# Gated linear attention and a SiLU block on one core: y of the first chunks by halves of the heads, the turnings of k behind the next chunk's, and a Silu and a sum one place later

## The chip, the cores and the metric

The kernel runs on one core of one Trainium2 chip. The time is that of one execution on the device in microseconds, taken as the median of the runs shown. Profiles show one execution each: TensorE (PE, and PEld for its weight loads), VectorE (DVE), ScalarE (ACT), GpSimd (POOL), and the DMA queues that SyncE (SP) and POOL issue.

## The reference

Two blocks follow each other. The first is a linear attention with a decaying state, for 4 batches, 8 heads, 768 steps and a head width of 48:

```python
for t in range(S):
    state = alpha[:, :, t, :, None] * state + np.einsum('bhd,bhe->bhde', k[:, :, t], v[:, :, t])
    y[:, :, t] = np.einsum('bhd,bhde->bhe', q[:, :, t], state)
```

Its y, laid out as 3072 tokens by 384, is x of the second block, with w_in of 384 x 2048 and w_out of 2048 x 384:

```python
h = x @ w_in
g = h * (1.0 / (1.0 + np.exp(-h)))
return (g @ w_out).astype(np.float32)
```

alpha and the weights arrive as 64-bit floats; everything is computed in fp32.

## The kernel before, in words

**Work and its tiles.** The sequence is cut into chunks of 128 steps, so there are 24 chunks n: 6 pieces of time (ci) by 4 batches (b). Chunks 0 to 3 are the first time piece (ci == 0): they have no earlier state to read. Four chunks make a group of 512 tokens for the second block; there are six groups.

**Attention of a chunk.** `bring` turns alpha, k and q with TensorE (`pe.transpose` against the identity, four per operand) into PSUM; the alpha part is copied by ACT (`al`, L759), the other two stay in PSUM. `products` and `quotient` (DVE) scan alpha in both directions and scale k and q by the running products, which gives `kp` and `qp`. `scores` multiplies them into two PSUM banks, one for the even and one for the odd head of each pair (u = 0, 1); ACT copies each bank to `g` (L854), and POOL zeroes what lies in the future with a select (L855), u = 0 first, then u = 1. `back` turns `kp` back (four transposes into a PSUM bank, an ACT copy to `kn`, L891). `values` computes y from `g` and v in 16 products with 32 columns of weights each, into one PSUM bank, and, where ci > 0, adds 12 products of the state with `qp`; ACT copies the bank to `xt` (L913), which is x of the second block. `states` multiplies `kn` with v into the new state; ACT copies it (L932) for ci == 0, DVE adds it otherwise (L930), and `scores` of the next time piece scales the old state on ACT (L874, four instructions).

**PSUM.** `ps_attn` hands out three banks in turn. `scores` takes two of them, `back`, `bring` (alpha), `values` and `states` one each; a bank is free again when its reader is done.

**Weights.** The 64-bit weights come in pieces (12 of w_in, then 16 of w_out), fetched by SP into four buffers `bits`. Converting a piece takes one ACT instruction (`up`, L654) and three of DVE (L670, L672, L673), after which the next piece is fetched. `convert(0, upto)`, in `start` shortened to `w(upto)`, converts pieces of w_in up to that count. The `up` of a piece is made with the piece before it, except that of the twelfth.

**Second block.** `enter_plain` computes four blocks of tokens of h directly, for the first two groups. From group 2 on, `enter(grp, pair)` computes a pair with a scheme of 20 block products (SUMS_X, SUMS_W, PRODUCTS) that are combined by DVE with additions and subtractions (L1008), over three PSUM banks a, b, c and a single SBUF buffer `part`, and ACT applies Silu in four instructions (L1005), each to two parts of a `g` tile. `leave` multiplies by w_out in seven products per half group (L1137 to L1163), with sums on DVE and stores L1115 and L1117.

**What sets the order.** The attention stages of step n and pieces of the second block are interleaved by hand: `start` writes out chunks 0 to 3, a loop with `fill` does the rest, calling `go_on` for one piece of second-block work at a time. Within that, TensorE's instructions keep the order of the program from the start to the end. DVE, ACT and POOL have theirs set by the framework's scheduler, except where `settled` or `tc.keep_in_program_order` pins an instruction. In `audit`, reductions over alpha and the weights (L723) are spread over the whole run on DVE; each waits for its own DMA.

**Lines that the texts below use.** `scores` calls `back(n)` at its end for n != 1 (L869); for chunk 1 `start` calls it after `values(0)`. The part of `start` for chunks 2 and 3 reads, shortened:

```python
scores(2); w(8); bring(3); w(9); values(2); states(2)
...
scores(3); bring(4); load(NIN + 4); w(12); values(3); states(3)
```

In `enter`, pair 0 of group 4 already has two orders of its own: `late_2` puts the subtraction from `s[2]` (L1050), which reads `part`, behind the addition to `s[6]`, and `late_3` one further subtraction behind its successor.

Of the kernel before, what the change touches and what calls it, by code (L numbers as in the profile page):

```python
# [355 lines left out]
def quotients(  # L356
# [237 lines left out]
    def combine(to, sa, a, sb, b):  # L594
        if sa == sb == 1:
            return dve.tensor_tensor(to, a, b, ALU.add)
        if sa == 1:
            return dve.tensor_tensor(to, a, b, ALU.subtract)
        if sb == 1:
            return dve.tensor_tensor(to, b, a, ALU.subtract)  # L600
        return dve.scalar_tensor_tensor(to, a, -1.0, b, ALU.mult, ALU.subtract)
# [227 lines left out]
    def scores(n):  # L829
        c = ctxs[n]  # L830
        ci, b = c["ci"], c["b"]
        ps = [ps_attn() for _ in range(2)]

        for j in (0, 2, 1, 3):
            for e in range(2 if n >= NA else 1):
                for u in range(2):
                    r = slice(64 * u, 64 * u + D)
                    at = slice(CH * e, CH * e + CH) if n >= NA else slice(0, C)  # L840
                    t = slice(CH * (e ^ j // 2) if n >= NA else 0, C)
                    pe.matmul(ps[u][at, j, t], lhsT=c["kp"][r, j, at], rhs=c["qp"][r, j, t],
                              start=True, stop=True)
        if n == 1:

            room = gpool.tile([128, 4, 2, TB], F32, name="g").rearrange("p a b n -> p (a b n)")
            c["room"] = room[:, 2 * NP * C :]
        g = (room[:, 0 : 2 * NP * C] if n == 1 else decayed).rearrange(
            "p (u j c) -> p u j c", u=2, j=NP)
        swapped = decayed.rearrange("p (o u j c) -> p o u j c", o=2, u=2, j=NP // 2)  # L850
        c["g"] = (lambda u, j: g[:, u, j, :]) if n < NA else (
            lambda u, j: swapped[:, j // 2, u, j % 2, :])
        for u in range(2 if n < NA else 0):
            settled(act.copy(g[:, u], ps[u]))  # L854
            gps.affine_select(g[:, u], g[:, u], pattern=[[0, NP], [1, C]], compare_op=ALU.is_ge,  # L855
                              fill=0.0, base=0, channel_multiplier=-1)
        if n >= NA:
            ps = [x.rearrange("p (o j) c -> p o j c", o=2) for x in ps]
            for u in range(2):
                act.copy(swapped[:, :, u, :, CH:], ps[u][:, :, :, CH:])  # L860
            for r, o in earlier:
                for u in range(2):
                    act.copy(swapped[r, o, u, :, 0:CH], ps[u][r, o, :, 0:CH])
            for at, half in ((CH, later), (0, earlier)):
                for r, o in half:
                    x = swapped[r, o].rearrange("p u j c -> p (u j) c")[:, :, at : at + CH]
                    gps.affine_select(x, x, pattern=[[0, NP], [1, CH]],  # L867
                                      compare_op=ALU.is_ge, fill=0.0, base=0, channel_multiplier=-1)
        if n != 1:  # L869
            back(n)  # L870
        if ci > 0:
            s = st[b].rearrange("p j u e -> p j (u e)")
            for j in range(NP):
                mul = act.mul(s[:, j], s[:, j], least[:, n, j : j + 1])  # L874
                if late or n == 6:
                    tc.keep_in_program_order(mul)
# [4 lines left out]
    def back(n):  # L881

        c = ctxs[n]
        if n >= NA or c["ci"] == NCH - 1:
            return
        ps_k = ps_attn()
        for j in range(NP):
            pe.transpose(ps_k[:, j, :], c["kp"][:, j, :], ident)
        c["kn"] = c.pop("room")[:, 0 : NP * C].rearrange("p (j c) -> p j c", j=NP) if (
            "room" in c) else work.tile([128, NP, C], F32, name="kn")  # L890
        settled(act.copy(c["kn"], ps_k))  # L891

    def values(n):

        c = ctxs[n]
        ci, b, g, qp = c["ci"], c["b"], c.pop("g"), c["qp"]
        vn = c["v"].rearrange("p (j u) d -> p j (u d)", u=2)
        s = st[b].rearrange("p j u e -> p j (u e)")
        py = ps_attn()
        todo = [(3 * j + i, vn[:, j, at : at + 32], g(u, j))  # L900
                for j in range(NP) for i, at, u in ((0, 0, 0), (1, 32, 0), (2, 80, 1))]
        todo += [(3 * j + 1, vn[:, j, 48:80], g(1, j)) for j in range(NP)]
        if ci > 0:
            todo += [(3 * j + i, s[:, j, 32 * i : 32 * i + 32], qp[:, j, :])
                     for j in range(NP) for i in range(3)]
        for i, (at, w, x) in enumerate(todo):
            t, at = divmod(at, 4)
            pe.matmul(py[32 * at : 32 * at + 32, t, :], lhsT=w, rhs=x, start=(i < 4),
                      stop=(i >= len(todo) - 4), skip_group_check=True)
        half, e = divmod(n, 2)  # L910
        if e == 0:
            xts[half] = xtp.tile([128, NKT, TB], F32, name="xt")
        settled(act.copy(xts[half][:, :, e * C : (e + 1) * C], py[:, 0:NKT]))  # L913
# [67 lines left out]
    def enter(grp, pair):  # L981
        g_tiles(grp, pair)
        halves = [gts[grp, h, pair] for h in range(2)]

        s = [halves[o % 2][:, o // 2] for o in range(8)]
        todo = iter(PRODUCTS)

        def new(i):
            return bank(i).rearrange("p (e n) -> p e n", e=2)

        def add(ps, first=False):
            w, x = next(todo)
            for e in range(2):
                pe.matmul(ps[:, e], lhsT=block_w(w)[:, 2 * pair + e], rhs=block_x(grp, x),
                          start=(first and e == 0), stop=(e == 1), skip_group_check=True)

        def copy(ps, to=None):
            if to is None:
                to = late["part"].tile([128, 2, TB], F32, name="part")
            act.copy(to, ps)  # L1000
            return to

        def silu(h, i):
            x = halves[h][:, i : i + 2]
            act.activation(x, x, AF.Silu)  # L1005

        def tt(to, a, b, op=ALU.add):
            dve.tensor_tensor(to, a, b, op)  # L1008

        a, b, c = [new(i) for i in range(3)]  # L1010
        add(a, True)
        copy(a, s[6])
        add(b, True)
        copy(b, s[2])
        add(c, True)
        tt(s[6], s[6], copy(c), ALU.subtract)
        yield
        add(c)
        copy(c, s[7])
        add(b)  # L1020
        copy(b, s[4])
        add(a)
        tt(s[7], s[7], copy(a), ALU.subtract)
        yield
        add(a)
        copy(a, s[5])
        add(b)
        copy(b, s[3])
        tt(s[5], s[5], s[3])
        add(c)  # L1030
        copy(c, s[0])
        yield
        add(a)
        tt(s[4], a, s[4])
        b = new(1)
        add(b, True)
        add(b)
        copy(b, s[1])
        yield
        c = new(2)  # L1040
        add(c, True)
        t = copy(c)
        late_2 = (grp, pair) == (4, 0)
        if not late_2:
            tt(s[2], s[2], t, ALU.subtract)
        a = new(0)
        add(a, True)
        tt(s[6], a, s[6])
        if late_2:
            tc.keep_in_program_order(dve.tensor_tensor(s[2], s[2], t, ALU.subtract))  # L1050
        silu(0, 2)
        add(b)
        tt(s[5], copy(b), s[5], ALU.subtract)
        yield
        add(c)
        tt(s[1], c, s[1])
        late_3 = (grp, pair) in ((2, 0), (4, 0))
        if not late_3:
            tt(s[3], s[1], s[3], ALU.subtract)
        a = new(0)  # L1060
        add(a, True)
        tt(s[2], a, s[2])
        if late_3:
            tt(s[3], s[1], s[3], ALU.subtract)
        add(b)
        tt(s[7], b, s[7])
        silu(1, 2)
        yield
        add(c)
        combine(s[1], -1, s[1], -1, s[0])  # L1070
        tt(s[0], c, s[0])
        silu(0, 0)
        a = new(0)
        add(a, True)
        tt(s[3], a, s[3])
        silu(1, 0)
        turn.append(turn.pop(0))
        for h in range(2):
            side_by_side(grp, h, pair)
        yield  # L1080
# [180 lines left out]
    def start():  # L1261
# [34 lines left out]
        scores(2)  # L1296
        w(8)
        bring(3)
        w(9)
        values(2)  # L1300
        states(2)
# [5 lines left out]
        w(11)  # L1307
        go_on()
        scores(3)
        bring(4)  # L1310
        load(NIN + 4)
        w(12)
        values(3)
        bridged = 4
        states(3)
# [120 lines left out]
```

## Time and profile before

| | us |
|---|---|
| median of three runs | 551.8 (551.37 to 552.56) |
| the profiled execution | 552.26 |
| its span, first to last instruction | 550.5 |
| PE busy | 539.8 |
| PEld busy | 493.0 |
| DVE busy | 446.3 |
| ACT busy | 209.1 |
| POOL busy | 79.7 |

By stretch, the busy time of PE is 46.0 of the first 50 us, 74.5 of the next 75, all of the 259 from 125 to 384, 14.8 of the 16 from 384 to 400, and 145.5 of the last 150.5. The granted TensorE clock is full throughout (0.999 in the mean).

How to read the lines: a row of the timeline has the start in us from the span's first instruction, the length, the engine, the line of the kernel, the operation, output <- inputs, the shapes and how many instructions are merged (x4). In square brackets stands the time for which the engine was idle before it, with what ended that wait; "issue" means that nothing in the profile ended it. A line of the view of waits has the waiting engine and line, what it waited for, and then the total in us, the number of waits and the longest. One fp32 product of TensorE appears as two records, each a weight load (LDWEIGHTS, on PEld) and a MATMUL (on PE). The operation of the helper that records all products has one line, L394, and that of the transposes L398; they are told apart by their tiles.

### The profile page before, as it was taken

What the parts mean: (1) busy time and instruction counts of PE and PEld (TensorE: products, weight loads), DVE (VectorE), ACT (ScalarE), POOL (GpSimd) and SP (SyncE); (2) the same over time, 40 slices, a digit from 0 to 9 for tenths busy, and PEclk for the clock granted to TensorE, in tenths of its full rate; (3) what the DMA queues carried; (4) which work ended last, traced back from release to release, by engine and by line L of the source; (5) the groups of instructions that cost most, each with busy time, mean ns of one, the idle gap of its engine ahead of it and who ended that gap; (6) DMA issues with size and microseconds to landing.
All of it is one profiled execution on the core that took longest, in us unless ns stands there. A gap on an engine that the chain in (4) does not pass through costs nothing. (4 is left out here: it accounts for less than half of the span.)

```text
span 550.5 us, 12714 instructions
## 1 busy us (share of the span) xinstructions
PE 539.8 (98%) x5068; PEld 493.0 (90%) x5068; DVE 446.3 (81%) x801; ACT 209.1 (38%) x466; POOL 79.7 (14%) x146
## 2 busy tenths in 40 slices
PE   8899999999999999999999999999999999999996
PEld 7788888998999899899999999998798999999996
DVE  5998789986989899997998986998884796945531
ACT  3655654213333433444444344353263341332100
POOL 4111001221222102201111111021121000001000
PEclk9999999999999999999999999999999999999999
DMA  9999761355445434545445653816732135500000
GB/s 214 301 238 221 205 187 43 87 147 138 109 119 138 116 96 107 131 127 157 123 133 157 166 147 90 219 33 152 192 126 85 54 100 166 172 11 19 13 29 26
DMA packets 99218, 70.11 MB, mean 127 GB/s; under 512 B 56272, under 2 KB 88656, under 8 KB 99152
## 3 DMA queue, kind: packets, MB, share of 16 engines
q1 hardware_dynamic: 97232, 65.30, 45.7%
q0 software_dynamic: 1920, 3.93, 2.0%
q8 instruction: 41, 0.67, 0.5%
q14 instruction: 25, 0.20, 0.1%
HBM read 61.34 MB, written 7.86 MB: 126 GB/s over the span
## 5 line engine op out<-in xcount | busy, mean ns | idle before, releaser
L394 PE MATMUL ps_o<-w_out,g 128*128 128x192 f32 x768 | 133.7, 328 | 0.6 <-DVE o L1117 0.6
L394 PEld LDWEIGHTS ps_o<-w_out,g 128*128 128x128 f32 x768 | 125.8, 190 | 3.1 <-DVE o L1117 0.8
L394 PE MATMUL ps_m<-xt,w_in 128*128 128x256 f32 x480 | 111.7, 381 | 0.9 <-ACT xt L913 0.5
L394 PEld LDWEIGHTS ps_m<-xt,w_in 128*128 128x128 f32 x480 | 89.7, 190 | 13.6 <-ACT part L1000 0.8
L394 PE MATMUL ps_o<-wt,g 128*128 128x192 f32 x576 | 99.7, 326 | 0.0
L394 PEld LDWEIGHTS ps_o<-wt,g 128*128 128x128 f32 x576 | 95.1, 190 | 1.5
L394 PE MATMUL ps_m<-xc,w_in 128*128 128x256 f32 x288 | 70.7, 382 | 0.0
L394 PEld LDWEIGHTS ps_m<-xc,w_in 128*128 128x128 f32 x288 | 53.7, 190 | 6.9 <-DVE g L1008 0.2
L1005 ACT ACTIVATE g<-g 128x1024 f32<-128x1024 f32 x32 | 33.1, 1056 | 66.1 <-DVE g L1008 66.0
L1108 DVE TENSOR_TENSOR g<-g 128x512 f32<-128x512 f32 x72 | 49.9, 704 | 7.9 <-PE ps_o L394 7.9
L867 POOL TENSOR_SCALAR_AFFINE_SELECT g<-g 64x256 f32<-64x256 f32 x64 | 36.9, 576 | 123.5 <-ACT g L860 104.5
L1120 POOL DMA_DIRECT2D out_dram<-o x40 | 22.0, 551 | 216.2 <-DVE o L1117 111.5
L1000 ACT COPY g<-ps_m 128x512 f32<-128x512 f32 x64 | 36.9, 586 | 41.4 <-PE ps_m L394 41.3
L394 PE MATMUL ps_m<-xc,wx 128*128 128x256 f32 x192 | 50.0, 383 | 0.0
L1008 DVE TENSOR_TENSOR g<-ps_m,g 128x512 f32<-128x512 f32 x56 | 37.3, 683 | 3.2 <-PE ps_m L394 2.7
L394 PEld LDWEIGHTS ps_m<-xc,wx 128*128 128x128 f32 x192 | 35.2, 190 | 4.0 <-issue 0.4
L770 DVE TENSOR_TENSOR_SCAN u<-al,one 128x516 f32<-128x516 f32 x24 | 29.7, 1239 | 7.0 <-ACT al L759 6.7
L973 ACT ACTIVATE g<-ps_m 128x512 f32<-128x512 f32 x32 | 19.0, 595 | 38.0 <-PE ps_m L394 37.7
L800 DVE TENSOR_TENSOR_SCAN p<-al,inv 128x516 f32<-128x516 f32 x24 | 30.2, 1260 | 0.9 <-PE ps_a L394 0.2
L723 DVE TENSOR_REDUCE seen<-bits 128x1 f32<-128x512 int32 (+1 forms) x33 | 26.3, 824 | 5.4 <-DMA bits<-in_moe_w_in_dram 5.4
L1117 DVE TENSOR_TENSOR o<-ps_o,u 128x192 f32<-128x192 f32 x24 | 8.5, 354 | 26.7 <-PE ps_o L394 24.8
L1000 ACT COPY part<-ps_m 128x512 f32<-128x512 f32 x32 | 18.9, 589 | 26.0 <-PE ps_m L394 21.0
(137 smaller groups left out, 655.7 us busy)
## 6 DMA issues: line engine op xcount, KB each, us to landing
bits<-in_moe_w_in_dram SPq DMA_DIRECT2D x24, 512.0 KB, 4.8
bits<-in_moe_w_out_dram SPq DMA_DIRECT2D x16, 384.0 KB, 3.8
at<-in_alpha_dram SPq DMA_DIRECT2D x64, 96.0 KB, 2.7
kt<-in_k_dram SPq DMA_DIRECT2D x64, 96.0 KB, 2.7
qt<-in_q_dram SPq DMA_DIRECT2D x64, 96.0 KB, 2.8
bits<-in_alpha_dram SPq DMA_DIRECT2D x9, 512.0 KB, 4.2
out_dram<-o POOLq DMA_DIRECT2D x40, 96.0 KB, 2.4
flips<-turn SPq DMA_DIRECT2D x12, 256.0 KB, 2.6
```

The source lines that it names most:

```text
L394: in_order(nc.tensor.matmul(*args, **kw))
L723: dve.tensor_reduce(seen[kind][which][:, i : i + 1], x, axis=AX, op=op, apply_absolute_value=True))
L770: settled(dve.tensor_tensor_scan(u[:, end - 1 :: -1], sg[:, end:0:-1], one[:, end:0:-1], 0.0, ALU.mult, ALU.add))
L800: settled(dve.tensor_tensor_scan(p[:, 0:end], sg[:, 0:end], iv[:, 0:end], 0.0, ALU.mult, ALU.add))
L867: gps.affine_select(x, x, pattern=[[0, NP], [1, CH]], compare_op=ALU.is_ge, fill=0.0, base=0, channel_multiplier=-1)
L973: settled(act.activation(gts[grp, h, pair][:, i : i + 2, q % 2, :], ps, AF.Silu))
L1000: act.copy(to, ps)
L1005: act.activation(x, x, AF.Silu)
L1008: dve.tensor_tensor(to, a, b, op)
L1108: dve.tensor_tensor(cells(grp, h, pair, *to), cells(grp, h, pair, *x), cells(grp, h, pair, *y), ALU.subtract)
L1117: dve.tensor_tensor(o, x, y, ALU.add)
L1120: (gps if grp < NG - 1 else nc.sync).dma_start(out[r : r + C, c * HO : (c + 1) * HO], o)
```

## The change

Four edits, in the diff below.

1. `values`, for ci == 0: the 16 products of y are listed anew. The parts are the same (for each of four pairs of heads j: columns 0, 32, 48 and 80 of v, the first two with g of u = 0, the last two with g of u = 1), but the eight of u = 0 come first, then the eight of u = 1. Four products in a row still go to four different quarters of the bank's rows.
2. `scores` no longer calls `back` for chunks 1, 2 and 3. `start` calls `back(2)` behind `bring(3)`, and `back(3)` behind `bring(4)`; chunk 1 is as it was.
3. In `start`, `w(12)` moves from behind `load(NIN + 4)` to ahead of `bring(4)`.
4. In `enter`, for group 4, pair 0 alone: the first Silu (of `s[4]` and `s[6]`) comes behind the copy of bank b and the subtraction from `s[5]` instead of ahead of them, and it and the sum into `s[1]` (`combine`, L601) are pinned to the order of the program.

How the instructions stand on each engine afterwards, from the two built programs:

- PE: in chunks 2 and 3 the four transposes of `kp` come behind the twelve of the next chunk's alpha, k and q. The products of y are in their new order. Nothing else differs.
- ACT: in chunk 2, `up`, `al`, `kn` instead of `kn`, `up`, `al`; in chunk 3, `up`, `al`, `kn` instead of `kn`, `al`, `up`, and of the four scalings of the state (L874) that came behind chunk 3's copies, one now stands ahead of the `xt` copy (L913) and one behind it. In group 4, pair 0, the copy to `part` comes ahead of the first Silu.
- DVE: in group 4, pair 0, L601 comes behind the transpose of alpha (L734) and a store's addition (L1117) instead of ahead of both. Near 55 us, one L1091 and one L672 change places.
- SP: one fetch of w_out comes ahead of the three loads of `load(NIN + 4)` instead of behind them.
- POOL: the same.

```diff
@@ scores
-        if n != 1:
+        if not 1 <= n <= 3:
             back(n)
@@ values
         todo += [(3 * j + 1, vn[:, j, 48:80], g(1, j)) for j in range(NP)]
+        if ci == 0:
+            at = (0, 32, 48, 80)
+            todo = [(3 * j + (i + 1) // 2, vn[:, j, at[i] : at[i] + 32], g(i // 2, j))
+                    for j, i in ((0, 0), (0, 1), (2, 0), (1, 0), (1, 1), (3, 0), (3, 1), (2, 1),
+                                 (0, 3), (0, 2), (1, 2), (3, 3), (1, 3), (2, 3), (2, 2), (3, 2))]
@@ enter
         def silu(h, i):
             x = halves[h][:, i : i + 2]
-            act.activation(x, x, AF.Silu)
+            return act.activation(x, x, AF.Silu)
...
         if late_2:
             tc.keep_in_program_order(dve.tensor_tensor(s[2], s[2], t, ALU.subtract))
-        silu(0, 2)
+        else:
+            silu(0, 2)
         add(b)
         tt(s[5], copy(b), s[5], ALU.subtract)
+        if late_2:
+            tc.keep_in_program_order(silu(0, 2))
         yield
...
         add(c)
-        combine(s[1], -1, s[1], -1, s[0])
+        total = combine(s[1], -1, s[1], -1, s[0])
+        if late_2:
+            tc.keep_in_program_order(total)
         tt(s[0], c, s[0])
@@ start
         bring(3)
+        back(2)
         w(9)
...
         scores(3)
+        w(12)
         bring(4)
+        back(3)
         load(NIN + 4)
-        w(12)
         values(3)
```

## The prediction

> **What bounds the kernel.** The page's first part comes first: TensorE's rows are busy for all but 2% of the span, so only time in which PE issues nothing can be won.
>
> ```profile
> PE 539.8 (98%) x5068; PEld 493.0 (90%) x5068; DVE 446.3 (81%) x801; ACT 209.1 (38%) x466; POOL 79.7 (14%) x146
> ```
>
> The chain that ended last shows one line of DVE and stops, so it does not help. I go to the view of waits (who waited, for whom: total us, times, longest) and look for PEld, the weight loads, with which PE's queue stops.
>
> ```profile
> PEld ps_a L394 <- POOL g L855: 1.3, 3, 0.7
> PEld ps_m L394 <- DVE g L1008: 1.0, 3, 0.6
> PEld ps_o L394 <- DVE o L1117: 0.8, 1, 0.8
> PEld ps_m L394 <- ACT part L1000: 0.8, 1, 0.8
> PEld ps_a L398 <- ACT g L854: 0.7, 2, 0.4
> ```
>
> These five are what the change can touch: 4.6 us, a ceiling. Two places hold nearly all of it: the start (18 to 47 us) and group 4, pair 0 (387 to 396 us). The timeline shows each. Chunk 2, weight loads (start, length, what; in brackets the idle time before and its releaser):
>
> ```profile
> 34.22 0.42 PEld L398 LDWEIGHTS ps_a<-ident,an 128*128 128x128 f32 x4 [0.38 <-ACT g L854]
> ...
> 35.68 0.14 PEld L394 LDWEIGHTS ps_a<-g,vn 128*32 128x32 f32 x4 [0.17 <-issue]
> 36.17 0.69 PEld L394 LDWEIGHTS ps_a<-g,vn 128*32 128x32 f32 x26 [0.35 <-POOL g L855]
> ...
> 36.87 0.58 PEld L394 LDWEIGHTS ps_a<-vn,kn 128*32 128x32 f32 x30
> ```
>
> Each fp32 product shows as two records, so y of a chunk is 32 records. Four are issued (35.68), then PE waits for the second half of the heads (the second select on POOL), and 28 are left behind that wait.
>
> **The change, part by part, against the profiled execution's own 552.26 us (span 550.5).**
>
> *1. Order of y, chunks 0 to 3.* Same 16 products, same columns of PE in turn; the eight of the first half come first, so 16 records instead of 28 stand behind the second select. An undisturbed y (394.00 to 394.90) issues 32 records in 0.90 us: 12 fewer are worth 0.34. Chunk 0 had no wait there: 0. Chunk 1 gains 0.34 at 18.3, but see its next stall:
>
> ```profile
> 20.21 0.23 PEld L394 LDWEIGHTS ps_a<-vn,g 128*32 128x32 f32 x13 [0.81 <-issue]
> ```
>
> That stall lies inside one tile's products, where no data can be late. If PE waits there for something that comes at a fixed time, the 0.34 turns into more waiting. The bounds are 0 and 0.34; I take 0, because the stall (0.81) is longer than the gain.
> The Trainium skill ("Runtime: NRT & Kernel Launch", section "Instruction fetch mechanics") says an engine's instructions are fetched ahead in 16 KiB blocks and that this is hidden by the pace of issue. If it holds here the stall is something else and may move along, making the sum 0.34 better; the 0.81 us of "issue" speaks against it.
>
> *2. Turnings of k (four transposes, one ACT copy) behind those of the next chunk, in chunks 2 and 3.* The 0.30 us that `an` lost waiting for a bank (34.22 against about 33.92) goes. Alone this buys nothing: what is late next is the second select at 36.12. PE now reaches the second half at about 35.8 and waits until 36.17 as before. Chunk 2 gains the 0.34 of part 1 only. ACT now has `up`, `al`, `kn` where it had `kn`, `up`, `al`: kn ends at about 36.2 instead of 35.15, and the states, its readers, start at about 36.6: covered by 0.4.
>
> *3. Chunk 3 arrives 0.34 earlier, and here the select can move.* Timeline, DVE and POOL:
>
> ```profile
> 44.08 0.69 DVE L673 CUSTOM_DVE_ANT_0 w_in<-w_in,up 128x1024 uint16<-128x1024 uint16 x1
> 44.69 0.42 DVE L670 TENSOR_SCALAR w_in<-bits 128x512 int32<-128x512 int32 x1
> 44.78 1.85 POOL L855 TENSOR_SCALAR_AFFINE_SELECT g<-g 128x512 f32<-128x512 f32 x2 [8.67 <-ACT g L854]
> 45.14 1.00 DVE L672 SCALAR_TENSOR_TENSOR w_in<-bits,w_in 128x512 int32<-128x512 int32 x1
> ...
> 45.55 1.08 POOL L855 TENSOR_SCALAR_AFFINE_SELECT g<-g 128x512 f32<-128x512 f32 x1
> ```
>
> L672 takes 1.00 here and 0.69 at 41.36; the selects of chunk 2 take 0.85 and 1.08 (34.23, 35.04) and those of 62.05, where DVE does nothing, 0.61 a piece. So they hold each other off in turn. From these rows: a held-off select ends 0.49 after the DVE instruction (46.63 after 46.14; 36.12 after 35.62), a held-off L672 0.54 after the select (35.62 after 35.08). DVE's own order here comes unbroken from 36.21 and does not move. In the new kernel the first select asks at 44.44, inside L673 and before L670. Whoever asked first goes first (at 94.52 the select waits for L619 and goes ahead of L620), so: select 1 ends 44.77 + 0.49 = 45.26, L670 0.27 later (0.42 less the 0.15 of overlap) at 45.53, select 2 at 46.02 instead of 46.63. PE, without the 0.30 and 0.34 earlier, is at the second half at about 46.0, resumes at 46.08 instead of 46.69 (0.61), with 0.34 less behind it: by the states PE is 0.95 ahead, chunk 2's share included. kn ends at about 46.4, just ahead of the states at 46.5. If DVE goes first instead, select 2 ends at 46.63 again, and 0.34 remains of the 0.95.
> The Trainium skill ("SBUF — State Buffer", section "Who interferes with whom") calls this an exclusive lock between the two engines, held for the whole instruction by whoever issues first. By that rule the select, asking first, gives 0.95; the row at 16.29, where a select and an L670 start together and L670 goes ahead, would leave 0.34.
>
> *4. What else moves there.* Piece 12 of w_in (three DVE instructions, one `up`) is written ahead of chunk 4's turnings; its `up` ends earlier, its last DVE instruction at about 47.4 instead of 47.48; PE's first use of that piece is at about 47.9. A fetch passes load(6) on SP's queue (three DMAs, an at 45.46, up to 1.3 later): chunk 6 is turned only after 77, free. In ACT's order one scaling of the state (L874, waits for DVE L773, 48.66) now stands ahead of the copy of x of chunk 3, which goes from 47.81 to about 49. PE reads that half in the middle of its 10.6 us block from 48.03, near 53: 3 us of cover; past it, each us costs one.
>
> *5. Pair 0 of group 4.* Timelines of PEld, DVE and ACT:
>
> ```profile
> 388.61 0.73 PEld L394 LDWEIGHTS ps_m<-xt,w_in 128*128 128x128 f32 x4 [0.83 <-ACT part L1000]
> ...
> 396.30 2.57 PEld L394 LDWEIGHTS ps_o<-w_out,g 128*128 128x128 f32 x16 [0.84 <-DVE o L1117]
> ```
>
> ```profile
> 386.91 0.68 DVE L1050 TENSOR_TENSOR g<-g,part 128x512 f32<-128x512 f32 x1
> ...
> 394.35 0.68 DVE L601 SCALAR_TENSOR_TENSOR g<-g 128x512 f32<-128x512 f32 x1
> 394.95 1.11 DVE L734 STREAM_TRANSPOSE al<-at 128x512 f32<-128x512 f32 x1
> 395.91 0.34 DVE L1117 TENSOR_TENSOR o<-ps_o,u 128x192 f32<-128x192 f32 x1
> ```
>
> ```profile
> 387.99 0.57 ACT L1000 COPY part<-ps_m 128x512 f32<-128x512 f32 x1
> ...
> 404.06 0.60 ACT L1000 COPY part<-ps_m 128x512 f32<-128x512 f32 x1
> ```
>
> The Silu no longer stands ahead of the copy at 387.99; what is late next is the single `part` buffer, free when L1050 ends (387.59). The copy starts at about 387.65, PE resumes at 388.27: 0.34, which PE carries only to the next wait, L1117. In DVE's new order L601 comes after L734 and L1117. L601 to L734 is a pitch of 0.60, so L1117 ends at 395.65, PE resumes at 395.71: 0.60 in all, the 0.34 inside it. L601's reader (L1008, 397.30) keeps its place, and so does the Silu's (L1091, 399.53). Then ACT: Silu, copies and scalings run without a pause from 398.00 to 404.67, started by DVE and not by PE. The bank that the copy at 404.06 frees is wanted by PE at 405.23; moved up by 0.60 it would be 404.63, but it comes free at 404.72, and the first load is no longer hidden (0.10). Left: 405.23 - 404.72 - 0.10 = 0.41. From 405.43 on ACT waits for PE again.
>
> **Sum:** 0.95 + 0.41 = 1.36: 550.9 for such an execution. The median of the runs shown (551.8) lies 0.46 below the profiled one, so the forecast for the median is **550.4**. From 48 to 384 I assume the shift is kept: PE shows no long wait there, and DVE's idle times end on PE (339.24: 2.24 us).
>
> **Rivals** (as medians). About 0.2%, 1.1 us or 550.7, is what a measurement of this kernel can tell from no change.
> - *DVE goes first in chunk 3.* For it: at 16.29 a select and an L670 start together and L670 wins. Against: here the select asks 0.2 us ahead. 0.34 + 0.41 = 0.75: 551.05.
> - *The stall at 20.2 moves along.* For it: its row names no releaser. Chunk 1's 0.34 then reaches chunk 2, whose select gets ahead of L670 as in part 3 (about 0.15 more): 1.85, 549.95.
> - *The early gain is eaten later* (or part 5 is): DVE, not PE, sets the pace up to 387, so an earlier PE only waits longer at L1008 (387.05). Against: DVE idles for PE at 339 to 341. 0.41 or 0.95 left: 551.4 or 550.85.
> - *Slower.* If the 0.81 at 20.2 is PE running out of instructions after a dense run (83 weight loads from 17.16), then y and states of chunks 2 and 3, now denser, stop likewise: 2 x 0.81 - 1.36 = +0.26, 552.05 (three stops: 552.9). It decides once a run is denser than chunk 1's. Against: 66.76 to 68.77 has 88 loads in 2 us and no stop.
>
> **Chances.** Forecast 0.45, DVE first 0.16, stall moves along 0.17, eaten later 0.13, slower 0.09. The forecast lies only 0.3 below the bound, so a third of it ends within 0.2%: faster 0.30 + 0.17 + 0.04 from the two middling cases = 0.51; slower beyond 0.2% needs the three stops, half of its case, 0.05; same 0.44. The range goes from the second rival less 0.4 (spread of the medians) to the third's upper value plus 0.2: 549.5 to 551.6.
>
> **What would show it.** Right: no PEld wait on ACT L854 at 34 and 44 us; y split 16/16 records around the select; chunk 3's second select ending near 46.0; L1117 ahead of L601 and PE resuming near 395.7 less the early shift; PE 1.3 us earlier from 405 on. Wrong: a select longer than before, PEld waits on kn (L891), new stalls by "issue", or PE's wait at 387.05 grown by the early gain.

## The result, and the profile after

| | before | after |
|---|---|---|
| median of 22 runs each, us | 551.88 (551.18 to 553.04) | 551.15 (550.52 to 553.07) |
| ratio, 95% interval | | 0.9985 (0.9978 to 0.9992) |
| a second time, both on one chip (e5 below): median | 551.12 | 550.11 |
| ratio, 95% interval | | 0.9982 (0.9973 to 0.9991) |
| the profiled execution; its span | 552.26; 550.5 | 551.14; 549.4 |

The change gains 0.7 to 1.0 us, under 0.2%. That is less than the 1.36 of the forecast, and by the bound set there it is "no change", though it stands clear of the noise. The kernel before has medians 0.7 apart on two chips (551.81 and 551.12 below), so below a time is set against those of the same chip alone, and across chips only ratios are compared.

The page's first part of the kernel after, and its view of waits (who waited, for whom: total us, times, longest):

```profile
PE 539.0 (98%) x5068; PEld 491.6 (89%) x5068; DVE 447.4 (81%) x801; ACT 208.7 (38%) x466; POOL 79.1 (14%) x146
```

```profile
PEld ps_a L394 <- issue: 13.0, 44, 1.4
...
PEld ps_a L394 <- POOL g L855: 1.2, 3, 0.6
...
PEld ps_a L398 <- ACT g L854: 0.8, 1, 0.8
...
PEld ps_o L394 <- DVE o L1127: 0.6, 1, 0.6
...
PEld ps_m L394 <- ACT part L1005: 0.5, 2, 0.3
```

(Lines from 903 on have moved by 5 to 10: L1117 is L1127, L1000 is L1005, L1008 is L1013.) In the view of waits before, the first of these rows was:

```profile
PEld ps_a L394 <- issue: 11.9, 43, 0.8
```

The two short waits for L854 have become one long one, L1127 and `part` are shorter, and the longest wait by "issue" has grown from 0.8 to 1.4. Where they lie, in the timeline of weight loads after:

```profile
33.52 0.42 PEld L398 LDWEIGHTS ps_a<-ident,an 128*128 128x128 f32 x4
...
35.42 0.81 PEld L394 LDWEIGHTS ps_a<-g,vn 128*32 128x32 f32 x32 [0.17 <-issue]
...
45.20 0.38 PEld L394 LDWEIGHTS ps_a<-g,vn 128*32 128x32 f32 x16 [0.17 <-POOL g L855]
46.20 0.38 PEld L394 LDWEIGHTS ps_a<-g,vn 128*32 128x32 f32 x16 [0.62 <-POOL g L855]
...
62.43 0.42 PEld L398 LDWEIGHTS ps_a<-ident,an 128*128 128x128 f32 x4 [0.77 <-ACT g L854]
```

`an` of the next chunk no longer waits at 34. Chunk 2's y runs through without any wait for the select (32 records, no cut), chunk 3's is cut 16 and 16, as meant. The long wait for L854 is new: it stands in chunk 4, at 62.43, where the kernel before had none.

To see where PE gains and loses, take the start of the same matmul in two traces; the difference is PE's **lead**. The columns are the places, in us of the trace of before; the values are in us against that trace (minus is earlier, a lead; the runs e1 to e12 come below). "First at 34" says which of two instructions started first in chunk 2, the select on POOL or DVE's L670:

| trace | first at 34 | 16 | 25 | 58 | 70 | 384.5 | 397 | 410 |
|---|---|---|---|---|---|---|---|---|
| after | POOL | -0.16 | +0.09 | -0.86 | -0.17 | +0.18 | -1.13 | -0.94 |
| e1, y alone | DVE | +0.10 | +0.09 | -0.76 | -0.50 | -0.45 | -1.44 | -1.44 |
| e2, turnings alone | POOL | +0.22 | -0.07 | -0.50 | -0.16 | +0.17 | +0.05 | +0.05 |
| e3, group 4 alone | DVE | +0.05 | +0.02 | +0.05 | +0.05 | +0.38 | -0.75 | -0.54 |
| e4, all but group 4 | DVE | +0.02 | +0.26 | -0.74 | -0.45 | -0.29 | -0.18 | -0.18 |
| e5, after again | DVE | -0.01 | -0.04 | -1.06 | -0.78 | -0.70 | -2.25 | -2.06 |
| e6, after, chunk 4's pieces later | POOL | -0.12 | -0.39 | -1.22 | -1.22 | +0.28 | -1.22 | -1.16 |
| e7, before, audit moved | POOL | -0.17 | +0.16 | -0.43 | 0.00 | +1.83 | +0.03 | +0.03 |
| e8, after, audit moved | DVE | -0.07 | +0.19 | -1.05 | -0.77 | +0.60 | -1.20 | -1.20 |
| e9, before, audit from step 21 | DVE | -0.13 | -0.10 | -0.13 | -0.12 | -0.07 | -1.87 | -1.87 |
| e10, e4 and that audit | POOL | +0.11 | -0.60 | -0.84 | -0.16 | +0.19 | -1.62 | -1.62 |
| e11, after and that audit | POOL | +0.15 | -0.15 | -0.95 | -0.26 | -0.21 | -2.01 | -2.01 |
| e12, chunk 1's y old | POOL | +0.11 | -0.19 | -0.99 | -0.30 | -0.29 | -1.35 | -1.35 |

(The values at 16 lie ahead of all edits: up to 0.2 is chance, the draw of a run.) The row "after" tells the story of its trace: 0.95 won from 25 to 58, 0.69 of it lost by 70, 0.35 more by 384, and then 1.1 won in group 4 (from 384.5 to 410).

### The profile page after: what moved, and what is told of

Same layout as the page of the kernel before. It is cut to its first block, busy times and chain, and to the rows that moved or that the text cites. A ratio compares the mean times of both kernels' runs of the same rounds, so it can differ in the third digit from the quotient of the medians.

```text
span 549.4 us, 12715 instructions
## 1 busy us (share of the span) xinstructions
PE 539.0 (98%) x5068; PEld 491.6 (89%) x5068; DVE 447.4 (81%) x801; ACT 208.7 (38%) x466; POOL 79.1 (14%) x146
## 5 line engine op out<-in xcount | busy, mean ns | idle before, releaser
L394 PEld LDWEIGHTS ps_m<-xt,w_in 128*128 128x128 f32 x480 | 89.5, 190 | 13.3 <-ACT xt L918 0.8
L1005 ACT COPY g<-ps_m 128x512 f32<-128x512 f32 x64 | 36.9, 587 | 41.6 <-PE ps_m L394 41.4
L1013 DVE TENSOR_TENSOR g<-ps_m,g 128x512 f32<-128x512 f32 x56 | 37.3, 684 | 3.2 <-PE ps_m L394 2.7
L800 DVE TENSOR_TENSOR_SCAN p<-al,inv 128x516 f32<-128x516 f32 x24 | 30.0, 1251 | 0.9 <-PE ps_a L394 0.3
L1005 ACT COPY part<-ps_m 128x512 f32<-128x512 f32 x32 | 18.9, 590 | 31.3 <-PE ps_m L394 25.6
L723 DVE TENSOR_REDUCE seen<-bits 128x1 f32<-128x512 int32 (+1 forms) x33 | 26.3, 821 | 5.1 <-DMA bits<-in_moe_w_in_dram 5.1
L1127 DVE TENSOR_TENSOR o<-ps_o,u 128x192 f32<-128x192 f32 x24 | 8.5, 354 | 26.7 <-PE ps_o L394 24.8
```

Of the source, the lines that this page charges most:

```text
L394: in_order(nc.tensor.matmul(*args, **kw))
L723: dve.tensor_reduce(seen[kind][which][:, i : i + 1], x, axis=AX, op=op, apply_absolute_value=True))
L800: settled(dve.tensor_tensor_scan(p[:, 0:end], sg[:, 0:end], iv[:, 0:end], 0.0, ALU.mult, ALU.add))
L1127: dve.tensor_tensor(o, x, y, ALU.add)
```

## The experiments

**e1 to e4: the parts, alone and together.** The edits are those of the diff above: e1 has only the one in `values`; e2 has `back(2)`, `back(3)` and `w(12)` moved; e3 has only the one in `enter`; e4 has e1's and e2's.

> Only the order of the products of y in chunks 0 to 3 is new; the turnings of k, the place of piece 12 and group 4 are as before. Theory K (as predicted: what is won in the first 48 us is kept to the end): chunks 2 and 3 restart behind the second select with 16 records instead of 28, 0.34 each at most, and since chunk 3 arrives 0.34 earlier it may win more there; 0.3 to 0.7 us faster than before in the median. Theory E (eaten): chunk 1's gain turns into a longer stall at 20.2 us (0.81 before, 1.2 to 1.4 here), the rest is gone by 62 us, because the weight loads of the next chunk's alpha wait there for ACT, which waits for DVE's weight pieces; 0.0 within 0.2, and the shift of PE against before is zero, but for what a run's DMAs do, between 125 and 384 us.

> Only the turnings of k behind the next chunk's in chunks 2 and 3, with piece 12 of w_in ahead; y and group 4 as before. Theory K: the waits for ACT at 34.2 and 44.8 us (0.30 each) go, but the second select is late next in both chunks, so nothing is won: 0.0 within 0.2. Theory E expects the same in the end. What tells more is the place: if the select on POOL is no longer held off (0.64 instead of 0.85 and 1.08 us), because DVE stands elsewhere when it asks, PE leads by 0.3 to 0.6 after 48 us; by E it has lost that by 64 us.

> Only the later Silu and the pinned sum in pair 0 of group 4; the first 384 us are as before. Theory K (as predicted): 0.34 at 388.6 and 0.26 at 396.3, of which 0.19 are lost at ACT's chain at 405: 0.41 faster. Theory E: all of the change's gain (0.73 in the medians) comes from here, 0.6 to 0.9 faster; in the trace 0.57 at 388.6, 0.28 at 396.3, less 0.19 at 405 (0.66), and the further 0.46 that the changed kernel won at 387.05 was DVE's passing its wait for a DMA at 373.9 sooner, which comes and goes with the run.

> The order of y and the moved turnings and piece 12, that is all of the change but group 4. Theory K: 0.95 faster (0.34 in chunk 2, 0.61 in chunk 3), kept to the end. Theory E: PE leads by 0.8 to 1.0 at 58 us, loses most of it at 62 (a new wait of about 0.5 to 0.8 for ACT's copies of the scores of chunk 4) and the rest on DVE's locks before 384; 0.0 to 0.2 faster.

Measured, against before on the same chip (551.81):

| | median | ratio, 95% interval |
|---|---|---|
| e1 | 551.55 | 0.9992 (0.9982 to 1.0002) |
| e2 | 551.69 | 0.9993 (0.9984 to 1.0002) |
| e3 | 551.31 | 0.9987 (0.9978 to 0.9996) |
| e4 | 551.79 | 0.9996 (0.9987 to 1.0005) |

By the ratios the start is worth 0.2 us (e4; not to be told from nothing, and at most 0.7 by the interval) and group 4 0.7 (e3; 0.2 to 1.2, which holds theory K's 0.41 too), about 0.9 together, as measured for the whole. So theory E is right about the sum: the start, counted at 0.95, does not arrive in full. The 0.95 is right in its place, though: e4 wins 1.00 from 25 to 58. Half of theory E fails as well: at 70 e4 still leads by 0.45, and most of what is left of that at 384.5 (0.29) goes at 387. The weight loads of e4 there:

```profile
386.95 0.73 PEld L394 LDWEIGHTS ps_m<-xt,wx 128*128 128x128 f32 x4 [0.79 <-DVE g L1013]
388.51 0.73 PEld L394 LDWEIGHTS ps_m<-xt,w_in 128*128 128x128 f32 x4 [0.83 <-ACT part L1005]
```

The first of these waits in the trace of before:

```profile
387.05 0.73 PEld L394 LDWEIGHTS ps_m<-xt,wx 128*128 128x128 f32 x4 [0.60 <-DVE g L1008]
```

PE came earlier and waited longer: DVE sets the time at 387, and DVE was hardly earlier (its subtraction L1050 starts at 386.81 in e4 and at 386.91 in before; why is told at e7). e1 shows how far a single trace can be trusted: without any edit in group 4 it wins 0.99 between 384.5 and 397, and its runs are not measurably faster.

**e5 and e6: the loss at 62.** e5 is the changed kernel unaltered; e6 has this edit in `fill`:

```diff
-            convert(1, 3 * (done - 6) // 2)
+            if (step, slot) > (5, 0):
+                convert(1, 3 * (done - 6) // 2)
```

> The changed kernel as it is, beside the three that follow, for a second trace of it and its time on the same chip. Theory E (the early gain is eaten at 62 us and after, group 4 pays): 0.5 to 0.8 faster than before. What repeats in the second trace belongs to the change: y 16 and 16 around the select, no wait of PE for ACT L854 at 34 and 44 us, the stall at 20.3 us longer than the 0.81 of before, and a lead of PE of 0.8 or more at 58 us that is under 0.3 at 70. What does not repeat (where DVE passes its waits for DMAs at 373 and 391 us) belongs to the run.

> The changed kernel with the pieces of w_out that the first filling (step 5, slot 0) converts put off to the next: two ACT instructions (up) and six of DVE fewer stand ahead of the copies of the scores of chunk 4. Theory E: the wait at 62.4 us is ACT's copies standing behind up, which waits for DVE's pieces; with those out of the way the wait goes and PE keeps its 0.8 to 0.9 past 70 us; at the end 0.3 to 0.8 faster than the changed kernel, unless DVE's later pieces, now three behind, hold back w_out or DVE eats the lead again by 387. If the wait at 62.4 stays, or another of the same size comes right behind it, the copies were not what was late.

Measured, on one chip with before at 551.12: e5 550.11 (0.9982, 0.9973 to 0.9991); e6 551.41 (1.0004, 0.9994 to 1.0013).

e5 keeps a lead of 0.78 at 70 (under 0.3 was expected) where the first trace of the same program kept 0.17. The two part at 34, where POOL's select and DVE's L670 want to start within hundredths of a microsecond. All engines' timeline of after, then of e5 (x2 is both selects):

```profile
34.33 1.41 POOL L855 TENSOR_SCALAR_AFFINE_SELECT g<-g 128x512 f32<-128x512 f32 x2 [16.23 <-ACT g L854]
...
34.36 0.89 DVE L670 TENSOR_SCALAR w_in<-bits 128x512 int32<-128x512 int32 x1
```

```profile
34.14 0.42 DVE L670 TENSOR_SCALAR w_in<-bits 128x512 int32<-128x512 int32 x1
34.19 1.90 POOL L855 TENSOR_SCALAR_AFFINE_SELECT g<-g 128x512 f32<-128x512 f32 x2 [15.95 <-ACT g L854]
```

By 0.03 us POOL goes first in after: both selects take 1.41, and L670 0.89 instead of 0.42. By 0.05 us DVE goes first in e5: the selects take 1.90. The Trainium skill ("SBUF — State Buffer", section "Who interferes with whom") says that who issues first holds the shared ports and the other blocks; these rows agree. POOL's going first is a trade and no gift. DVE's pieces of weights, late by 0.47 after the first order, stay late: at 60.3 DVE is 0.39 behind before in after, and 0.22 ahead in e5. ACT's `up` waits for them, and the copies of chunk 4's scores stand behind `up` on ACT. The timelines of after and e5 again:

```profile
60.87 0.55 ACT L654 ACTIVATE up<-bits 128x384 int32<-128x384 uint32 x1 [1.00 <-DVE w_out L673]
...
61.80 1.07 ACT L854 COPY g<-ps_a 128x512 f32<-128x512 f32 x2
...
62.43 0.42 PEld L398 LDWEIGHTS ps_a<-ident,an 128*128 128x128 f32 x4 [0.77 <-ACT g L854]
```

```profile
60.25 0.56 ACT L654 ACTIVATE up<-bits 128x384 int32<-128x384 uint32 x1 [1.00 <-DVE w_out L673]
...
61.19 1.07 ACT L854 COPY g<-ps_a 128x512 f32<-128x512 f32 x2
...
61.82 0.42 PEld L398 LDWEIGHTS ps_a<-ident,an 128*128 128x128 f32 x4 [0.36 <-ACT g L854]
```

The table bears it out: of the traces with y and turnings new (e6 apart, which moves these pieces), those with POOL first (after, e10, e11, e12) lose 0.68 or 0.69 between 58 and 70, those with DVE first (e4, e5, e8) 0.28 or 0.29. No run forces the order at 34, so that it decides how late the pieces are is read from these rows and the table alone.

e6 takes the pieces out of the way. Its lead of 1.22 goes through 62 unharmed, as theory E wanted. But the pieces that were put off are in the way one chunk later, in the line below, where PE waits 1.60, twice as long, and the time is longer than the changed kernel's where 0.3 to 0.8 less was expected. So the pieces are confirmed as the cause of the wait at 62, and this move finds no slack for them:

```profile
81.05 0.42 PEld L398 LDWEIGHTS ps_a<-ident,an 128*128 128x128 f32 x4 [1.60 <-ACT g L854]
```

**e7 to e11: who makes PE wait in group 4.** The audit's reductions (L723) wait on DVE for their fetches. This line of DVE's timeline before, and the same wait for the next piece (0.81 at 391.36), are what the prediction took as given:

```profile
373.87 1.28 DVE L723 TENSOR_REDUCE seen<-bits 128x1 f32<-128x512 int32 x2 [1.84 <-DMA bits<-in_moe_w_in_dram]
```

SP issues this fetch as soon as DVE's reductions ahead of it are done (in before the last of them runs from 368.35 for 0.69). SP's timeline of before, then of e4:

```profile
369.07 0.35 SPq L709 DMA_DIRECT2D bits<-in_moe_w_in_dram  x1
```

```profile
368.64 0.35 SPq L709 DMA_DIRECT2D bits<-in_moe_w_in_dram  x1
```

In the nine traces without a move of the audit, the issue is earlier or later than in before by as much as PE is at 370, to 0.06 (e5: 0.72 with PE 0.78 ahead; e4: 0.43 with 0.45; e3: 0.35 later with PE 0.38 behind). So a lead of PE does reach DVE here. What is drawn from trace to trace comes after: from issue to landing it is 4.28 (after) to 4.86 (e4), 4.78 in before, and from there to L1050 12.8, or 13.0 to 13.3 where POOL's selects hold DVE off. In e4 both draws are the worst of the nine and take up 0.33 of the 0.43; its timeline of all engines:

```profile
378.50 2.17 POOL L867 TENSOR_SCALAR_AFFINE_SELECT g<-g 64x256 f32<-64x256 f32 x3 [10.16 <-ACT g L860]
378.52 0.59 DVE L1159 TENSOR_TENSOR u<-u,u 128x192 f32<-128x192 f32 x1
379.03 1.43 DVE L800 TENSOR_TENSOR_SCAN p<-al,inv 128x516 f32<-128x516 f32 x1
```

(In after L1159, there L1164, takes 0.36 and L800 1.23.)

e7 (on before) and e8 (on after) move all of these reductions by one slot; e9 (on before), e10 (on e4) and e11 (on after) only those from step 21 on, which begins with the one that waits at 373.87:

```diff
-        if at % 2 == 0 and step > 3 * GB + 2:
+        if at % 2 == 1 and step > 3 * GB + 2:              # e7, e8
+        if at % 2 == (step > 20) and step > 3 * GB + 2:    # e9, e10, e11
```

> The kernel before, with each reduction of the audit moved from the even slots of a step to the odd ones; no part of the change. DVE's wait of 1.84 us at 373.9, for a piece that could be fetched only 4.8 us earlier, is what makes DVE late for pair 0 of group 4 by this theory. The moved ones stand 10 to 17 DVE instructions elsewhere, so that the fetch lies over more work. Theory D (DVE's lateness sets PE's waits at 387, 388.6 and 396): PE waits less than 0.2 at 387.05 and less than 0.4 at 396, 0.6 to 1.5 faster than before. Rival: the three waits are made by the order of ACT and by the one buffer part; then they stay, and so does the time, within 0.3.

> The changed kernel with the same move of the audit. Theory D: whatever lead PE has at 384 is kept through group 4 and the wait at 395.2 (0.55) goes or shrinks: 0.4 to 1.2 faster than the changed kernel. If the later Silu and the pinned sum were worth their time only because DVE came late there, the difference between this and the kernel before with the moved audit is under 0.4; if they pay by themselves it is 0.6 or more.

> The kernel before, with the audit's reductions moved to the odd slots from step 21 on only, that is from the one whose wait at 373.9 us holds DVE on; nothing of the change. Theory D (DVE's waits for the audit's fetches, 1.84 at 373.9 and 0.81 at 391.4, set PE's three waits in pair 0 of group 4): DVE passes 374 and 391 without a wait, PE's waits at 387.05, 388.6 and 396.3 (0.36, 0.59, 0.83 above the usual pitch) shrink to under 0.3 in sum, and the time is 0.8 to 1.6 faster than before, since the two new waits of the kernel that moved all of them (0.48 at 271, 0.86 at 363) lie ahead of step 21. If the end of the program gets longer again (6.1 instead of 5.1 to 5.5 us from the last matmul to the end), 0.7 of it is lost there. Rival: the waits are ACT's and the one buffer part's; then 388.6 at least stays.

> The order of y and the moved turnings and piece 12, without the edit of group 4, with the audit moved from step 21 on. By itself, without the audit's move, this part was worth nothing (ratio 0.9996). Theory D: it was worth nothing because at 387 PE took over DVE's time, whatever lead it brought; with DVE early there, the lead of 0.4 to 0.8 at 360 us comes through: 0.4 to 0.8 faster than the kernel before with the same audit. If the two are within 0.2 the lead is lost elsewhere.

> The changed kernel with the audit moved from step 21 on. Theory D: the edit of group 4 gained by working around a late DVE; with DVE early it adds 0.0 to 0.3 to the kernel with the start's edits and the same audit, and PE waits under 0.2 at 395. Against the changed kernel: 0.3 to 0.8 faster, unless the end of the program grows; 1.2 to 2.0 faster than before, the best so far.

Measured, e7 and e8 beside before at 551.12, e9 to e11 beside before at 551.17 on another chip:

| | median (lowest to highest) | ratio, 95% interval |
|---|---|---|
| e7 | 552.87 (552.08 to 553.11) | 1.0028 (1.0017 to 1.0038) |
| e8 | 552.40 (551.83 to 554.06) | 1.0027 (1.0017 to 1.0036) |
| e9 | 550.48 (550.10 to 550.77) | 0.9985 (0.9976 to 0.9994) |
| e10 | 549.79 (549.61 to 550.41) | 0.9974 (0.9964 to 0.9984) |
| e11 | 550.03 (549.69 to 550.41) | 0.9978 (0.9969 to 0.9987) |

e7 and e8 miss what was expected of the time: they are slower than before. The reason is elsewhere: new waits, in e7 at 271.3 (0.61) and 363.6 (0.96), with which PE falls 1.8 behind by 384.5, and 6.1 us from the last matmul to the end in place of 5.1 to 5.5. Nor does the pair show whether the edits pay by themselves: e8 is 0.47 faster than e7 by the medians and 0.06 by the ratios. Their group 4 does what theory D says, and so does that of e9. DVE's and PE's lines in e9's timeline:

```profile
383.17 0.68 DVE L1050 TENSOR_TENSOR g<-g,part 128x512 f32<-128x512 f32 x1
383.76 1.27 DVE L723 TENSOR_REDUCE seen<-bits 128x1 f32<-128x512 int32 x2
...
386.40 0.84 PEld L394 LDWEIGHTS ps_m<-xt,wx 128*128 128x128 f32 x4
...
387.27 0.84 PEld L394 LDWEIGHTS ps_m<-xt,w_in 128*128 128x128 f32 x4
...
394.43 1.60 PEld L394 LDWEIGHTS ps_o<-w_out,g 128*128 128x128 f32 x10 [0.20 <-issue]
```

L1050 starts at 383.17 instead of 386.91, and all three waits of PE are gone, the one for `part` at 388.6 too, though ACT's order, Silu ahead of the copy, is the old one. The rival (ACT and the one buffer) is out. (One wait of DVE for a fetch, 2.9, is left, at 448, where PE waits for nobody.) In all five traces with the audit moved, e7 to e11, PE gains 1.80 from 384.5 to 397, whether the edit of group 4 is in or not: that is the sum of the three waits of before (0.36, 0.59 and 0.83 above the usual pitch, 1.78). The edit alone gets part of it. In after, with the old place of the audit:

```profile
387.76 0.73 PEld L394 LDWEIGHTS ps_m<-xt,w_in 128*128 128x128 f32 x4 [0.26 <-ACT part L1005]
...
390.76 0.69 DVE L723 TENSOR_REDUCE seen<-bits 128x1 f32<-128x512 int32 x1 [1.06 <-DMA bits<-in_moe_w_in_dram]
...
395.18 0.95 PEld L394 LDWEIGHTS ps_o<-w_out,g 128*128 128x128 f32 x6 [0.55 <-DVE o L1127]
```

The gain in time of e9, 0.8 by the ratio, is at the lower end of what was expected; the profiled run of before had one of the worst draws in group 4 (next section), so that its 1.80 need not be that of every run.

e10 against e9 is the test of the start: 0.69 faster in the medians and 0.6 by the ratios, five of e10's nine runs below the lowest of e9's eleven. So on top of the moved audit the start's edits pay, within what theory D expected. That they pay because of the moved audit is not shown: e4 against before was 0.02 in the medians and 0.2 by the ratio, but its interval reaches 0.7. Nor does the trace show where they pay: the profiled run of e10, one of its slowest (550.37), lost 0.44 from 25 to 70 and is 0.25 behind that of e9 at 410.

e11 against e10 is the test of group 4's edit: 0.24 slower, with ranges that cover each other; with DVE early it gains nothing that these runs show, where alone it had 0.7. Against the change, e11 was expected 0.3 to 0.8 faster; by the ratios it is 0.2 to 0.4 (0.9978 against 0.9982 and 0.9985), not clear of the intervals. e10, y and turnings with the audit moved from step 21 on and group 4 as it was, has the lowest median, not to be told from e11's: 1.4 us faster than before by median and ratio, where the change had 0.8 and 1.0 by its two ratios.

**e12: chunk 1.** The changed kernel with `if ci == 0 and b != 1:` in `values`.

> The changed kernel with chunk 1's y in its old order; chunks 0, 2 and 3 in the new one. As predicted (what chunk 1 gains is waited for again at 20.2 us): within 0.2 of the changed kernel; the wait inside the tile at 20.2 us is 0.5 to 0.9 (as in the traces with the old order: 0.81, 0.51, 0.77) instead of 1.1 to 1.4, and ends at the same 20.1 to 20.5 us. Rival (the gain of chunk 1 counts): 0.3 slower than the changed kernel.

Measured 550.36, 0.9986 (0.9977 to 0.9995), against 0.9985 and 0.9982 for the change. No difference shows, as predicted, but the interval is 1 us wide and holds the rival's 0.3 as well; the traces tell more. The wait in e12 is 0.49 and ends at 20.02, a little ahead of the bounds that were set. In the mean of the six traces with chunk 1's old order the wait is 0.76 and PE goes on at 20.18; in the mean of the eight with the new order it is 1.07 (0.43 to 1.41) and PE goes on at 20.14. What the order wins there is waited for again. With the new order, in after:

```profile
18.50 0.40 PEld L394 LDWEIGHTS ps_a<-vn,g 128*32 128x32 f32 x19
20.31 0.23 PEld L394 LDWEIGHTS ps_a<-vn,g 128*32 128x32 f32 x13 [1.40 <-issue]
```

## Why the prediction was right, and why its size was not

The time fell into the range (549.5 to 551.6) and, at 0.73 us, into the case of no change, which was given 0.44; the gain is about half of the 1.36. By its own steps:

1. *Order of y.* Right. Where PE waits for the second select, y is cut into 16 and 16 records, and chunk 1's gain is nothing: the stall in its states grows by 0.3 in the mean of the traces (e12).
2. *Turnings.* Half right. The waits for `an` go. "Alone this buys nothing" holds in the time (e2: 0.9993). But chunk 2 was not the fixed thing that it was taken for: in after it gained 0.77 instead of 0.34, with POOL first, in e5 0.41.
3. *Chunk 3, whoever asks first goes first.* Right where chunk 2 ran as assumed: e5's second restart is at 46.05 (46.08 was forecast), and chunk 3 gains 0.6 in e4, e5 and e8. In after DVE was 0.66 behind by then, the selects met L672 and L673 in place of L670, and the gain was 0.2. The lead won from 25 to 58 is 0.95 in after, 1.00 in e4 and 1.02 in e5, and the forecast was 0.95; in after that is luck, 0.77 and 0.2 for the 0.34 and 0.61 of the forecast. In the others it is 1.24 (e8), 0.8 (e6, e11, e12) and 0.24 (e10, where PE waits 0.64 at 37.65 for a piece of w_in).
4. *"Free".* **Wrong.** The select's right of way was counted as a gain alone. DVE pays for it, ACT waits for DVE, and the next copies of the scores are late: 0.69 lost at 62 where POOL went first in chunk 2, 0.28 where DVE did (e6 apart). The step looked at the last piece of w_in and the copy of x, not at the pieces of w_out behind them.
5. *Pair 0 of group 4.* The edit's own terms are right: in e3, from 387.5 on, PE gains 0.35 at 388.6 and 0.32 at 396.3 and gives back 0.21 at 405, 0.46 in sum, where 0.34, 0.26, 0.19 and 0.41 were forecast; e3's runs, with 0.2 to 1.2, do not contradict it. But they stood on DVE's time of one trace, and a late one: its fetch took 4.78 to land, the second longest of nine, and DVE's scan L800 took 1.43 because POOL's select had begun 0.25 ahead of it (1.23 in after, e1, e3, e5 and e6). L1050 began anywhere from 385.53 (e5) to 386.93 (e2). Of the 1.4 between these two, 0.85 is PE's own lead or lag, handed on by the issue of the fetch; the rest is draw. The draws are worth up to 1 us for PE at 387 to 396: with the same code there, e1 wins 0.99 from 384.5 to 397 and e4 loses 0.1.
6. *"From 48 to 384 I assume the shift is kept", and the sum 0.95 + 0.41.* **The step that failed.** The seven traces with y and turnings new (e6 apart) keep from 25 to 70 between 0.96 (e8) and less than nothing (e10: 0.44 lost), 0.35 in the mean, and e4's runs give 0.2. Between 210 and 260 after, e2, e3 and e10 lose a third of a microsecond (in after a scan of DVE at 211 takes 1.46 for 1.23, beside POOL's selects); e3 has none of the start's edits, so this is a draw and not their price. At 387 PE takes over DVE's time. The prediction's third rival, an earlier PE that only waits longer there, was given 0.13: e4 does so (0.79 for 0.60). But it is no rule, since DVE's time moves with PE's by the issue of the fetch: e5, 0.78 ahead at 370, has L1050 1.38 earlier. The prediction's argument against this rival, that DVE idles for PE at 339, so holds as far as the fetch; the landing and the selects behind it, up to 1 us, it left out. With 0.41 left it would have been 551.4; 551.15 was measured.

The slower rival, PE out of instructions in chunks 2 and 3, did not come: no trace has such a stall there.

Open stays why some traces lose a third at 210 to 260 and others do not; where e10's runs win their 0.6 over e9's; and how often each order comes in runs without a trace. Of the eight traces with y and turnings new, POOL went first in five (after, e6, e10, e11, e12), which is too few to price it.

## What to carry to other kernels

A lead won early is worth what the next waits of the bounding engine let through: walk down the trace to each later place where that engine waits for another, and ask whether that other one gets earlier too; one that waits for a transfer does if the transfer is issued earlier. Where two engines take turns at a shared port, a gain of the one can be a debt of the other; follow the debtor to whoever waits for it next. When several waits lie close together, look for the one late engine behind them: here a reduction that checks the inputs and that nobody waits for until the end, reached by DVE 3.0 us after the issue of a fetch that takes 4.8 to land, made PE wait three times. Moving it brought 0.8 by the ratio where the edit around these waits brought 0.7, and with it in place that edit has no gain that the runs show.

## What was not expected of the hardware

PE's stall at 20.2 us stands at one instruction, not at one time or one tile's data: in all fourteen traces the 32 records of that chunk's states are cut into 19 and 13, at the same weight load counted from the start, whatever the order of y ahead of them. The wait is between 0.43 (e10) and 1.41 us (e8). In each trace the instruction queue moves its only packet of that stretch just before: in before from 17.14 for 1.47 us, and PE goes on at 20.21, 1.60 after its end; in the others 1.30 to 1.56 after. The DMA engines are busy nearly all that time (the digits of the first line are tenths, as on a page), here in after, 17 to 21 us:

```profile
DMA  9999999999999999999999789699998998999999
...
q8 instruction: 1, 0.02, 2.3%
```

This points to PE running out of instructions there. The Trainium skill ("Runtime: NRT & Kernel Launch", section "Instruction fetch mechanics") has the next 16 KiB fetched while the present ones run and calls the cost mostly hidden; if it is the fetch, it is not hidden here. That is not shown: it rests on this coincidence in fourteen traces, the fetch was not taken away, the view does not say which engine a packet is for, and the queue's next packet in before (24.14, 0.99 us) has no such stall behind it.
